# Row scatters issued behind GpSimd's product, and a tail of expert slots without conditions

## The chip, the cores and the metric

The kernel runs on one core of one Trainium2 chip. A core has five engines with instruction queues of their own: TensorE (PE, matrix products), VectorE (DVE), ScalarE (ACT), GpSimd (POOL) and SyncE (SP, which here issues DMAs). They meet through semaphores. The metric is the time of one execution on the device in microseconds, and the kernel before takes 1265.65 us (median of three runs, 1261.61 to 1265.8).

## The reference

Attention that keeps only the 32 largest scores of each row, and behind it a mixture of eight experts of which every row uses one:

```python
batch, heads, seq, dim = 8, 8, 576, 64
scores = (q @ k.T) / sqrt(dim)
kth    = 32nd largest score of each row
scores = where(scores >= kth, scores, -1e9)
x      = softmax(scores) @ v                  # 4608 rows of 512

logits = x @ w_gate + modality_bias[modality_id]
e      = argmax(logits)                       # one of 8 experts per row
gate   = softmax(logits)[e]
out    = gate * (relu(x @ w1[e]) @ w2[e])     # w1: 512x1024, w2: 1024x512
```

How many rows an expert gets is known only while the kernel runs.

## The kernel before, in words

**Attention.** The scores are worked off in 288 tiles of 128 query rows by 576 keys, 36 tiles for each of the eight batches. A Python loop over steps `i` writes the program; the work of one tile is spread over a dozen steps, and in each step every engine gets its share for another tile. There are no due times: what stands in an engine's queue is the order in which this loop calls the functions.

In a step, DVE first merges the candidates of the tile before (L386 to L388), between them takes the eight largest values of seven slices of a new tile (L375, the line with most time on DVE), looks through a product that GpSimd made (`find`, L417), picks the 32nd value of three tiles in every third step (L424 to L426, below a "pick step"), and ends with `keep` (L437): the comparison of the scores with the 32nd value times their exponentials, 128x576, into `P`. The first instruction of a step on DVE is therefore the L386 MAX8, and the time from one L386 MAX8 to the next is the length of a step.

GpSimd in a step: `gate` (L460) reads one number of the `P` that `keep` wrote at the end of the step before, and so holds the queue back until then; `pool_y` (L413) multiplies the scores by a sign mask `K` into `y`, 128x576, which DVE's `find` takes in the next step; `below` (L400) waits for DVE's merge L388 and makes a number that ACT needs for the next mask. In every third step `small` (L394) follows, and in one step of nine `fill` (L325).

**Rows on their way to the experts.** When a batch has its attention output, `route` chooses each row's expert and `send` (L590) scatters the rows to a buffer `xs` in HBM, grouped by expert: five indirect DMAs on GpSimd's queue for each batch, `send` of a first piece, a pause, of the second, and so on, so one in each of five steps. Each is followed by a one-element memset (L516). They are handed out through the list `side`, which a step empties (up to four entries, or up to a pause) together with DVE's small work: ahead of the step's `gate` and `pool_y`. Only the first batch goes through the list `sends` at the end of a step.

**Experts.** 256 rows of one expert make a slot. During attention PE gets matrix products of slots between those of attention (`moe`), after a budget per step (`STEP`) that is written out by the program and knows nothing of the run. A slot's result goes to the output by two more indirect DMAs on GpSimd, `put` (L792), which are issued two steps after the result, from the list `puts` at the end of a step.

**The tail.** What is left after attention are whole slots on PE (`slot`): 8 x 12 products for the hidden layer (L997), 2 x 24 for the output (L1013), a scaling on ACT into `ot` (L1018) and a scatter on GpSimd (L1019) for each half. `slot(n)` computes slot n-1 and fetches and prepares slot n: it loads rows and weights, splits them in two parts, and transposes the rows (L968) between the halves. One slot is computed before the conditions begin. Then the number of slots that are left, `nrem`, is read into a register of every engine (L1289), and 25 nested conditions (L1290) follow, each with a slot in it; a last slot that fetches nothing stands behind them. In this input 19 slots have rows, numbers 0 to 18: the first 13 run beside attention, and 13 to 18 in the tail. So four conditions hold, and the fifth does not: there every engine jumps over the bodies of 21. At the end the condition `bad > 0` (L1365) guards a slow version of the whole kernel, for inputs in which the search for the 32nd value fails; it isn't run here.

Of the kernel before, what the change touches and what calls it, by code (L numbers as in the profile page):

```python
# [12 lines left out]
I32 = mybir.dt.int32  # L13
AF = mybir.ActivationFunctionType
OP = mybir.AluOpType
# [57 lines left out]
def kernel(  # L73
# [12 lines left out]
    nc = tc.nc  # L86
    V, A, G, PE, SP = nc.vector, nc.scalar, nc.gpsimd, nc.tensor, nc.sync
    B, H, S, D = q.shape
    E, Dm, F = w1.shape
    N = B * S  # L90
# [5 lines left out]
    SLOT = 256  # L96
    LCAP = N + SLOT
    MAXSLOT = -(-N // SLOT) + E - 1

    const = ctx.enter_context(tc.tile_pool(name="const", bufs=1))  # L100
# [16 lines left out]
    PAUSE = lambda: None  # L117
# [292 lines left out]
    def pool_y(i):  # L410
        t = T[i]
        t["y"] = wk.tile([128, S], FT, name="y", bufs=YB)
        G.tensor_tensor(t["y"], t["S"], t["K"], op=OP.mult)  # L413
# [408 lines left out]
    side = deque()  # L822
    rush = deque()
    moe = deque()
    sends = deque()
    puts = deque()
    avs = deque()
    xev = deque()
    seen = [0]
    nslot = [0]  # L830

    def ready(n, whole):
        pick, rows, done, tok = sched(n, whole)
        for f in pick + done + rows + tok:
            f()
        for g in range(4):
            load_w1(n, g)
        for g in range(4):
            load_w2(n, g)
# [66 lines left out]
    bd_ = const.tile([128, 4], FT, name="bad")  # L906
# [73 lines left out]
    def choose(s):  # L980
        pick, rows, done, tok = sched(s, False)
        later[s] = rows + tok
        for f in pick + done:
            f()
# [4 lines left out]
    def slot(n):  # L989

        if n is not None:
            fetch(n)
        for f in range(FC):
            ps = acc([128, SLOT])
            for c in range(KC):
                for x, (a, b) in enumerate(TERMS):
                    PE.matmul(ps, w1s[a][:, c, f * 128:(f + 1) * 128], xgs[b][:, c, :],  # L997
                              start=(c == 0 and x == 0), stop=(c == KC - 1 and x == 2))
            A.activation(hs[0][:, f, :], ps, AF.Relu)
            V.scalar_tensor_tensor(hs[1][:, f, :], ps, 0.0, hs[0][:, f, :].bitcast(FT), op0=OP.max, op1=OP.subtract)  # L1000
            if f % 2 == 0:
                split_w2(f // 2)
            if n is not None:
                if f == 0:
                    for g in range(4):
                        load_w1(n, g)
                if f % 2 == 0:
                    load_w2(n, f // 2)
        for t in range(2):
            py = acc([128, Dm])  # L1010
            for f in range(FC):
                for x, (a, b) in enumerate(TERMS):
                    PE.matmul(py, hs[a][:, f, t * 128:(t + 1) * 128], w2s[b][:, f, :],  # L1013
                              start=(f == 0 and x == 0), stop=(f == FC - 1 and x == 2))
                if t == 0 and f % 2 == 1 and n is not None:
                    split_w1(f // 2)
            ot = const.tile([128, Dm], FT, name="ot", bufs=2)
            A.activation(ot, py, AF.Copy, scale=gt[:, t:t + 1])  # L1018
            apart(G.indirect_dma_start(  # L1019
                out=out[:, :], out_offset=bass.IndirectOffsetOnAxis(ap=tk[:, t:t + 1], axis=0),  # L1020
                in_=ot, in_offset=None, bounds_check=N - 1, oob_is_err=False), outs)
            if t == 0 and n is not None:
                turn_rows(n)
                choose(n + 1)
        if n is not None:
            of_rows(n)

# [19 lines left out]
    store = []  # L1047
    for i in range(LAST):
# [62 lines left out]
        if 0 <= b1 < B:  # L1111
            if r == 0:
                chore.extend(recip(b1, den[b1 % 2]))
            rl, rx = (RL, RX) if FAST <= b1 < B - 1 else (RLF, RXF)
            if r == rl[0]:
                rows_of[b1] = logits(b1, xTs(b1))
                cost += COST["logits"]
            if r == rl[1]:
                logit_rows(b1, rows_of[b1], lgb[b1 % 2])
                cost += COST["xrow"]  # L1120
            if r in rx:
                xrow(b1, rx.index(r), xTs(b1), x5)
                cost += COST["xrow"]
            if r == rl[1] + 2:
                steps, store = route(lgb[b1 % 2], bias_all[:, b1], ohb[b1 % 2], x5, int(0 < b1 < B - 1))
                side.extend(steps)

                def done(n=b1 + 1):
                    seen[0] = n * S
                    fresh.clear()  # L1130
                if b1 == 0:
                    side.extend([store.pop(), done])
            if r == max(rl[1], rx[4]) + (1 if b1 == 0 else 2):
                if b1 == 0:
                    sends.extend(f for f in store if f is not PAUSE)
                else:
                    side.extend(store + [done])
        u = i - (TL + 1)
        if avs:
            c, f = avs.popleft()  # L1140
            f()
            cost += c
        if ok(u) and role(u) in (3, 7, 8):
            f = av(u // 9, role(u), xTs(u // 36)[(u // 9) % HP])
# [13 lines left out]
        while seen[0] and spare_pe > 0:  # L1158
# [4 lines left out]
            c, f, new = moe[0]  # L1163
# [25 lines left out]
        for x in range(RN if rush else 0):  # L1189
            f = rush.popleft() if rush else PAUSE  # L1190
# [6 lines left out]
        for x in range(SN - len(small_)):  # L1197
            f = side.popleft() if side and not rush else PAUSE
# [10 lines left out]
        if ok(i) and len(c_) > 1:  # L1209
            n = min(len(c_) - 1, HOLD)  # L1210
# [11 lines left out]
            gate(i - 1 - LR)  # L1222
        if ok(i - LY):
            pool_y(i - LY)
        if ok(i - 1):
            below(i - 1)
        if ok(i - 2) and (i - 2) % 3 == 2:
            small(i - 4)
        if j == 5 and p + 1 < NPAIR:
            fill(p + 1, qbd[(p + 1) % 2])  # L1230
        if sends and seen[0]:
            sends.popleft()()
        for x in puts:
            x[0] -= 1
        while puts and puts[0][0] <= 0:
            puts.popleft()[1]()
        if i == CLOSE:
            alone[0] = True
            S0 = nslot[0]
# [15 lines left out]
        rush.popleft()()  # L1255
    while side:
        side.popleft()()


    while moe:  # L1260
# [12 lines left out]
        first.popleft()()  # L1273
    of_rows(S0)
    choose(S0 + 1)
    nl = const.tile([1, E], FT, name="nl")
    ni = const.tile([1, E], I32, name="ni")
    ns = const.tile([1, 1], FT, name="ns")
    V.tensor_tensor(nl, base[0:1, :], roff[0:1, :], op=OP.subtract)
    V.tensor_scalar(ni, nl, float(SLOT - 1), None, op0=OP.add)  # L1280
    V.tensor_scalar(ni, ni, SLOT.bit_length() - 1, None, op0=OP.arith_shift_right)
    V.tensor_copy(nl, ni)
    V.tensor_reduce(ns, nl, axis=AX.X, op=OP.add)
    nremi = const.tile([1, 1], I32, name="nrem")
    V.tensor_copy(nremi, ns)
    slot(S0 + 1)

    bad = nc.values_load(badi[:, :], min_val=0, max_val=256)
    nrem = nc.values_load(nremi[:, :], min_val=0, max_val=MAXSLOT)  # L1289
    with ExitStack() as nest:  # L1290
        for x in range(MAXSLOT):
            nest.enter_context(tc.If(nrem > x))
            slot(S0 + 2 + x)
    slot(None)
    att.close()

# [22 lines left out]
    def slow():  # L1319
        Pb[:] = [wk.tile([128, 2 * S], FT, name=f"P{i}", bufs=1) for i in range(2)]  # L1320
        outs.clear()
        PR.clear()
        reset_state()
        for x in (scat, reads, fresh):
            x.clear()
        with tc.For_i(0, B, 1) as b:
            dn = den[0]
            sb = wk.tile([128, 1, 5, E], FT, name="sl_b", bufs=1)
            bias_of(*load_mod(b, 1), 1, sb)
            for hp in range(HP):  # L1330
                load(hp, "kqv", b)
                for part in "tkq":
                    prep(hp, part)
                    flush()
                fill(hp, qbd[0])
                for j in range(9):
                    qk(j, hp, qbd[0])
                    sevac(j)
                    r = role(j)
                    slow_tile(j, dn[:, hp, r:r + 1])  # L1340
                    trans(j)
                    evac(j)
                    if r in (3, 7, 8):
                        for _, f in av(hp, r, xTs(0)[hp]):
                            f()
                        xev.popleft()()
            for f in recip(0, dn):
                f()
            L = logits(0, xTs(0))
            while xev:  # L1350
                xev.popleft()()
            logit_rows(0, L, lgb[0])
            flush()
            for c in range(5):
                xrow(0, c, xTs(0), x5)
                flush()
            for part in route(lgb[0], sb[:, 0], ohb[0], x5):
                for f in part:
                    f()
        with tc.For_i(0, MAXSLOT, 1):  # L1360
            ready(0, False)
            for _, f, _ in expert(0, True, False, False, False):
                f()

    with tc.If(bad > 0):  # L1365
        slow()


# [28 lines left out]
```

## Time and profile before

| | |
|---|---|
| median of three runs | 1265.65 us |
| the profiled execution | 1264.55 us |
| span of its trace | 1262.9 us |
| PE busy | 1179.7 us, 93% |
| DVE busy | 1145.9 us, 91% |
| ACT busy | 990.4 us, 78% |
| POOL busy | 681.4 us, 54% |
| granted PE clock, mean | 0.975 |

The span runs from the first to the last instruction; the profiled execution took 1.65 us more than its span. PE and DVE are both busy nearly all the time, but not in the same stretches: attention ends at about 1060 us, behind it DVE has little to do, and from 1105 to 1222 us PE is busy without a gap. Busy shares over the whole span say nothing about which of the two sets the time in a stretch; that is read from what they wait for. A row of a timeline gives the start, the length, the engine, the line, the operation and its tiles, and in brackets how long the engine had been idle before it and what ended that.

### The profile page before, as it was taken

To read this page: it belongs to the slowest core of one execution; us is meant where nothing else is said; L and a number is where in the kernel's file an instruction comes from. 1 tells how busy PE (TensorE), PEld (TensorE's weight loads), DVE (VectorE), ACT (ScalarE), POOL (GpSimd) and SP (SyncE) were. 2 spreads that over 40 slices of the span, in tenths; PEclk is the share of its full clock that TensorE was granted. 3 is DMA by queue.
4 is the path that set the end of the run, shared out by engine and by line. 5 is a ranking of instruction groups with operands and counts; after the bars stand their busy time and mean duration, and the time that the engine had idled before them with its cause. 6 is when DMAs were issued, how large, how long until landed. Compare 5 with 4: busy or idle time off the path is not lost. (4 is left out here: it accounts for less than half of the span.)

```text
span 1262.9 us, 28647 instructions
## 1 busy us (share of the span) xinstructions
PE 1179.7 (93%) x7962; PEld 923.5 (73%) x7962; DVE 1145.9 (91%) x5914; ACT 990.4 (78%) x2014; POOL 681.4 (54%) x1253
## 2 busy tenths in 40 slices
PE   8888888999988999999999999999999999999985
PEld 6667666777766777677777777787778775699885
DVE  6999999999999999999999999999999995477751
ACT  4999987889888988888889888988889875256442
POOL 5888866555574557554755566546655572210110
PEclk6999998999999999999999999999999999999998
DMA  4663337655356755655556666666666524577550
GB/s 100 156 185 84 85 84 199 175 154 161 84 134 183 207 132 148 182 149 151 176 152 182 161 182 163 183 167 176 171 185 176 140 67 133 187 254 270 179 174 15
DMA packets 204340, 197.26 MB, mean 156 GB/s; under 512 B 104413, under 2 KB 151533, under 8 KB 204160
## 3 DMA queue, kind: packets, MB, share of 16 engines
q1 hardware_dynamic: 196880, 175.92, 50.7%
q0 software_dynamic: 6080, 19.00, 4.1%
q8 instruction: 69, 1.13, 0.4%
q14 instruction: 111, 0.91, 0.2%
q10 hardware_dynamic: 1200, 0.30, 0.1%
HBM read 118.63 MB, written 24.23 MB: 113 GB/s over the span
## 5 line engine op out<-in xcount | busy, mean ns | idle before, releaser
L375 DVE MAX8 cand<-Ssb 128x8 f32<-128x82 f32 (+1 forms) x2016 | 433.1, 233 | 5.5 <-ACT Ssb L368 5.5
L413 POOL TENSOR_TENSOR y<-Ssb,K 128x576 f32<-128x576 f32 x288 | 369.7, 1284 | 4.3 <-ACT K L407 4.0
L407 ACT ACTIVATE K<-Ssb,n 128x576 bf16<-128x576 f32 x288 | 227.3, 789 | 36.1 <-POOL y L413 35.0
L363 PE MATMUL S<-ks,qs 128*128 128x288 f32 x992 | 221.8, 346 | 25.7 <-ACT Ssb L368 24.2
L368 ACT ACTIVATE Ssb<-S 128x576 f32<-128x576 f32 x284 | 185.6, 654 | 73.5 <-PE S L363 31.6
L417 DVE MAX8 mg<-y 128x8 f32<-128x576 f32 x288 | 215.1, 747 | 5.5 <-POOL y L413 5.5
L765 PE MATMUL E<-xgT,w1b 128*128 128x256 f32 x816 | 199.9, 388 | 11.3 <-ACT hT L769 9.1
L363 PEld LDWEIGHTS S<-ks,qs 128*128 128x128 f32 x992 | 151.8, 191 | 75.5 <-ACT Ssb L368 41.7
L437 DVE SCALAR_TENSOR_TENSOR P<-Ssb,kth,ex 128x576 f32<-128x576 f32 x230 | 201.8, 877 | 1.6 <-ACT ex L431 1.3
L431 ACT ACTIVATE ex<-Ssb,sm 128x576 f32<-128x576 f32 x256 | 199.9, 781 | 0.0
L479 ACT ACTIVATE PT<-T 128x640 f32<-128x640 f32 (+1 forms) x288 | 190.7, 662 | 6.4 <-PE T L471 6.4
L777 PE MATMUL E<-w2b,hT 128*128 128x512 f32 x400 | 187.3, 597 | 2.1 <-ACT hT L769 2.0
L765 PEld LDWEIGHTS E<-xgT,w1b 128*128 128x128 f32 x816 | 150.7, 193 | 36.5 <-ACT hT L769 12.2
L471 PE MATMUL T<-idf,P 128*128 128x128 f32 x1152 | 170.9, 276 | 6.1 <-ACT P L456 5.8
L460 POOL TENSOR_SCALAR spare<-P 1x1 f32<-1x1 f32 x230 | 46.7, 203 | 203.4 <-DVE mg L386 184.6
L499 PE MATMUL X<-PT,vm 128*64 128x256 f32 (+1 forms) x1536 | 147.1, 334 | 2.8 <-ACT st L277 1.5
L471 PEld LDWEIGHTS T<-idf,P 128*128 128x128 f32 x1152 | 138.0, 142 | 14.9 <-ACT P L456 10.4
L400 POOL TENSOR_SCALAR n<-mg 128x1 f32<-128x1 f32 x288 | 72.4, 251 | 106.1 <-DVE mg L388 98.2
L499 PEld LDWEIGHTS X<-PT,vm 128*64 128x64 f32 x1536 | 88.7, 138 | 48.6 <-issue 10.7
L777 PEld LDWEIGHTS E<-w2b,hT 128*128 128x128 f32 x400 | 70.6, 190 | 63.0 <-issue 57.7
L1019 POOL DMA_INDIRECT out_dram<-ot,tk x12 | 12.0, 998 | 105.0 <-ACT ot L1018 105.0
L903 PE MATMUL E<-onesb 128*128 128x256 bf16 x412 | 61.9, 292 | 2.8 <-ACT K L407 1.6
(234 smaller groups left out, 2231.5 us busy)
## 6 DMA issues: line engine op xcount, KB each, us to landing
w1b<-in_moe_w_dram SPq DMA_DIRECT2D x76, 512.0 KB
w2b<-in_moe_w_dram SPq DMA_DIRECT2D x76, 512.0 KB
ks<-st SPq DMA_DIRECT2D x62, 288.0 KB
ks<-st SPq DMA_DIRECT2D x62, 256.0 KB
qs<-st SPq DMA_DIRECT2D x124, 128.0 KB
xg<-xs SPq DMA_DIRECT2D x19, 516.0 KB
km<-in_k_dram SPq DMA_DIRECT2D x64, 128.0 KB
vm<-in_v_dram SPq DMA_DIRECT2D x32, 256.0 KB
```

The costliest lines, as they stand in the source:

```text
L363: PE.matmul(ps[:, hf, :288], l, m, start=(n == 0), stop=(n == len(terms) - 1))
L375: return [lambda s=s: V.max(c[:, s * 8:s * 8 + 8], T[i]["S"][:, bnd[s]:bnd[s + 1]]) for s in range(NSUB)]
L407: A.activation(t["K"], t["S"], AF.Sign, scale=2.0 ** -24 - 1.0, bias=t["n"][:, 1, i % 3:i % 3 + 1], accum_out=t["n"][:, 0, i % 3:i % 3 + 1])
L413: G.tensor_tensor(t["y"], t["S"], t["K"], op=OP.mult)
L417: V.max(t["mg"][:, i % 3, 24:32], t["y"])
L431: A.activation(t["ex"], t["S"], AF.Exp, bias=t["s"][:, i % 3:i % 3 + 1])
L437: V.scalar_tensor_tensor(t["P"], t["S"], kth[:, i:i + 1], t["ex"], op0=OP.is_ge, op1=OP.mult, accum_out=dn)
L471: PE.transpose(T[i]["pt"][:, x, :], (Pm if c == 4 else Pb[c % 2])[:, h * 512 + x * 128:h * 512 + x * 128 + 128], idf)
L479: A.activation(o, T[i]["pt"][:, :n], AF.Copy)
L499: PE.matmul(o.rearrange("p (a b) -> p a b", a=2) if j < 8 else o, l, r, start=(c == 0), stop=(c == 4))
L765: PE.matmul(ps[:, f % 2], w1b[:, c, f * 128:(f + 1) * 128], xgT[:, c, :], start=(c == 0), stop=(c == KC - 1))
L777: PE.matmul(o["py"], hT[:, f, t * 128:(t + 1) * 128], w2b[:, f, :], start=(f == 0), stop=(f == FC - 1))
```

## The change

Two edits. The first concerns GpSimd's queue in attention: the scatters of batches 1 to 7 are no longer issued where `side` hands them out, but put in a list `posted`, and one entry of `posted`, `sends` or `puts` is issued in a step, right behind `pool_y` and ahead of `below`. So a `put` that is due in the steps of the scatters comes after them.

The second concerns the tail: slots up to number 18 (`SURE`) are written out without a condition. Behind the last slot one condition, `more > 0`, guards a loop over the slots that could be left and, in it, the slow version; `more` is the number of rows that are left plus `bad`. The computation is the same.

```diff
+    posted = deque()
...
-                choose(n + 1)
+                if n < SURE:
+                    choose(n + 1)
...
-                    side.extend(store + [done])
+                    side.extend([f if f is PAUSE else (lambda f=f: posted.append(f)) for f in store[:-1]] +
+                                [store[-1], done])
...
         if ok(i - LY):
             pool_y(i - LY)
+        for x in puts:
+            x[0] -= 1
+        if posted:
+            posted.popleft()()
+        elif sends and seen[0]:
+            sends.popleft()()
+        elif puts and puts[0][0] <= 0:
+            puts.popleft()[1]()
         if ok(i - 1):
             below(i - 1)
         if ok(i - 2) and (i - 2) % 3 == 2:
             small(i - 4)
         if j == 5 and p + 1 < NPAIR:
             fill(p + 1, qbd[(p + 1) % 2])
-        if sends and seen[0]:
-            sends.popleft()()
-        for x in puts:
-            x[0] -= 1
-        while puts and puts[0][0] <= 0:
-            puts.popleft()[1]()
...
+    SURE = max(N // SLOT, S0 + 1)
+    for n in range(S0 + 1, SURE):
+        slot(n)
     nl = const.tile([1, E], FT, name="nl")
...
+    V.tensor_tensor(ns, ns, bd_[0:1, 3:4], op=OP.add)
+    morei = const.tile([1, 1], I32, name="more")
+    V.tensor_copy(morei, ns)
+    slot(SURE)
     bad = nc.values_load(badi[:, :], min_val=0, max_val=256)
-    nrem = nc.values_load(nremi[:, :], min_val=0, max_val=MAXSLOT)
-    with ExitStack() as nest:
-        for x in range(MAXSLOT):
-            nest.enter_context(tc.If(nrem > x))
-            slot(S0 + 2 + x)
+    more = nc.values_load(morei[:, :], min_val=0, max_val=N + 256)
     slot(None)
...
-    with tc.If(bad > 0):
-        slow()
+    with tc.If(more > 0):
+        with tc.For_i(0, MAXSLOT - SURE - 1, 1):
+            ready(0, False)
+            for _, f, _ in expert(0, True, False, False, False):
+                f()
+        with tc.If(bad > 0):
+            slow()
```

On GpSimd's queue, the steps in which batch 5 is scattered, before (L460 is `gate`, L413 the product, L400 `below`, L590 a scatter of rows, L792 a scatter of results):

```order
L590 DMA xs<-x_152,dest 38912x516
L516 MEMSET spare 1x1
L460 TENSOR_SCALAR spare<-P_119 1x1
L413 TENSOR_TENSOR y<-Ssb,K 128x576
L400 TENSOR_SCALAR n<-mg 128x1
L792 DMA out_dram<-ot,stok_130 4608x512
L516 MEMSET spare 1x1
L590 DMA xs<-x_152,dest 38912x516
L516 MEMSET spare 1x1
L460 TENSOR_SCALAR spare<-P_119 1x1
L413 TENSOR_TENSOR y<-Ssb,K 128x576
```

The same steps of the changed kernel:

```order
L460 TENSOR_SCALAR spare<-P_119 1x1
L413 TENSOR_TENSOR y<-Ssb,K 128x576
L590 DMA xs<-x_152,dest 38912x516
L516 MEMSET spare 1x1
L400 TENSOR_SCALAR n<-mg 128x1
L460 TENSOR_SCALAR spare<-P_119 1x1
L413 TENSOR_TENSOR y<-Ssb,K 128x576
L590 DMA xs<-x_152,dest 38912x516
L516 MEMSET spare 1x1
L400 TENSOR_SCALAR n<-mg 128x1
```

The first scatter moved from ahead of `gate` to between the product and `below`, and the scatter of results no longer stands in these two steps. The queues of PE, DVE, ACT and SP are the same in both kernels up to the tail.

On PE's queue, the place of the fifth condition, which does not hold here; behind it in the program stand 21 bodies, and then the slot that fetches nothing. Before:

```order
L1013 MATMUL X<-w2l,hh 128x512
L1013 MATMUL X<-w2h,hl 128x512
L1290 COMPARE_AND_BRANCH
L997 MATMUL X<-xgh,w1h 128x256
L997 MATMUL X<-xgl,w1h 128x256
...
L1013 MATMUL X<-w2h,hl 128x512
L1290 UNCONDITIONAL_BRANCH x26
L997 MATMUL X<-xgh,w1h 128x256
```

And in the changed kernel, between the slot that fetches number 18 and the one that fetches nothing:

```order
L1014 MATMUL X<-w2l,hh 128x512
L1014 MATMUL X<-w2h,hl 128x512
L1294 TENSOR_LOAD badi
L1295 TENSOR_LOAD more
L998 MATMUL X<-xgh,w1h 128x256
L998 MATMUL X<-xgl,w1h 128x256
```

The jump between the two slots is gone, and two register loads, which stood ahead of the first condition, stand in its place. The remaining conditional jump of the tail, over the loop and the slow version, comes behind the last product, where the one over the slow version was.

## Rows read from the trace of the kernel before

**Rows 1.** Stretches: start:end, length, busy us (and instructions) of PE, PEld, DVE, ACT, POOL, ...
```profile
349.20:481.00 131.80, 120.74 (x853) 93.50 (x852) 129.76 (x712) 113.32 (x232) 75.43 (x143) 0.97 0.61 165
618.00:749.70 131.70, 128.23 (x856) 98.28 (x855) 130.91 (x704) 114.69 (x236) 78.61 (x153) 1.00 0.61 169
749.70:881.00 131.30, 129.19 (x865) 99.58 (x864) 129.20 (x704) 114.70 (x238) 79.61 (x153) 1.00 0.61 170
```

**Rows 2.** Groups of DVE, 349.2 to 1045 us: busy us, mean ns | idle before, releaser
```profile
L437 DVE SCALAR_TENSOR_TENSOR P<-Ssb,kth,ex 128x576 f32<-128x576 f32 x168 | 144.2, 858 | 0.0
L417 DVE MAX8 mg<-y 128x8 f32<-128x576 f32 x189 | 141.5, 749 | 5.5 <-POOL y L413 5.5
```

**Rows 3.** Timeline of DVE, first instruction of a step: start, length, line, tiles
```profile
480.83 0.21 DVE L386 MAX8 mg<-cand 128x8 f32<-128x56 f32 x1
...
500.74 0.21 DVE L386 MAX8 mg<-cand 128x8 f32<-128x56 f32 x1
...
877.84 0.21 DVE L386 MAX8 mg<-cand 128x8 f32<-128x56 f32 x1
...
897.17 0.21 DVE L386 MAX8 mg<-cand 128x8 f32<-128x56 f32 x1
...
911.74 0.21 DVE L386 MAX8 mg<-cand 128x8 f32<-128x56 f32 x1
...
924.81 0.21 DVE L386 MAX8 mg<-cand 128x8 f32<-128x56 f32 x1
...
928.45 0.21 DVE L386 MAX8 mg<-cand 128x8 f32<-128x56 f32 x1
...
934.73 0.22 DVE L386 MAX8 mg<-cand 128x8 f32<-128x56 f32 x1
...
938.75 0.22 DVE L386 MAX8 mg<-cand 128x8 f32<-128x56 f32 x1
```

**Rows 4.** Timeline of POOL, 876 to 897 us, where batch 5 is scattered
```profile
876.70 0.19 POOL L400 TENSOR_SCALAR n<-mg 128x1 f32<-128x1 f32 x1 [1.00 <-DVE mg L388]
877.16 1.68 POOL L590 DMA_INDIRECT xs<-x,dest  x1 [0.28 <-issue]
...
879.18 1.27 POOL L413 TENSOR_TENSOR y<-Ssb,K 128x576 f32<-128x576 f32 x1
...
884.03 1.81 POOL L413 TENSOR_TENSOR y<-Ssb,K 128x576 f32<-128x576 f32 x1
...
895.34 1.28 POOL L413 TENSOR_TENSOR y<-Ssb,K 128x576 f32<-128x576 f32 x1
```

**Rows 5.** Timeline of DVE in the same stretch
```profile
877.11 0.80 DVE L437 SCALAR_TENSOR_TENSOR P<-Ssb,kth,ex 128x576 f32<-128x576 f32 x1
...
885.88 0.76 DVE L417 MAX8 mg<-y 128x8 f32<-128x576 f32 x1 [0.44 <-POOL y L413]
...
895.41 1.83 DVE L437 SCALAR_TENSOR_TENSOR P<-Ssb,kth,ex 128x576 f32<-128x576 f32 x1
```

**Rows 6.** Timeline of all engines, 482 to 485 us
```profile
482.60 0.98 POOL L590 DMA_INDIRECT xs<-x,dest  x1 [0.21 <-DVE cand L375]
...
483.24 0.80 DVE L437 SCALAR_TENSOR_TENSOR P<-Ssb,kth,ex 128x576 f32<-128x576 f32 x1
```

**Rows 7.** Timeline of ACT in the tail: the scaling of each half of a slot
```profile
1129.03 0.69 ACT L1018 ACTIVATE ot<-X,gt 128x512 f32<-128x512 f32 x1 [4.68 <-issue]
1146.10 0.69 ACT L1018 ACTIVATE ot<-X,gt 128x512 f32<-128x512 f32 x1 [1.38 <-PE X L1013]
...
1222.34 0.69 ACT L1018 ACTIVATE ot<-X,gt 128x512 f32<-128x512 f32 x1 [4.59 <-issue]
1244.34 0.69 ACT L1018 ACTIVATE ot<-X,gt 128x512 f32<-128x512 f32 x1 [5.16 <-PE X L1013]
```

**Rows 8.** Timeline of PE, the start of the last slot
```profile
1225.44 0.39 PE L997 MATMUL X<-xgh,w1h 128*128 128x256 f32 x1 [3.19 <-ACTq L1290]
```

**Rows 9.** Instructions of line 1290: queue, count, ns min/median/max, first and last start
```profile
L1290 PEldq COMPARE_BRANCH  x6: 65/76/3425, 1126.0 to 1222.4; - x6
```

More of the change, by code (lines that the diff above doesn't have):

```diff
@@ L1257 @@
         side.popleft()()
+        while posted:
+            posted.popleft()()
     while moe:
@@ L1275 @@
     choose(S0 + 1)
+    SURE = max(N // SLOT, S0 + 1)
+    for n in range(S0 + 1, SURE):
+        slot(n)
     nl = const.tile([1, E], FT, name="nl")
-    ni = const.tile([1, E], I32, name="ni")
     ns = const.tile([1, 1], FT, name="ns")
     V.tensor_tensor(nl, base[0:1, :], roff[0:1, :], op=OP.subtract)
-    V.tensor_scalar(ni, nl, float(SLOT - 1), None, op0=OP.add)
-    V.tensor_scalar(ni, ni, SLOT.bit_length() - 1, None, op0=OP.arith_shift_right)
-    V.tensor_copy(nl, ni)
     V.tensor_reduce(ns, nl, axis=AX.X, op=OP.add)
-    nremi = const.tile([1, 1], I32, name="nrem")
-    V.tensor_copy(nremi, ns)
-    slot(S0 + 1)
+    V.tensor_tensor(ns, ns, bd_[0:1, 3:4], op=OP.add)
+    morei = const.tile([1, 1], I32, name="more")
+    V.tensor_copy(morei, ns)
+    slot(SURE)
     bad = nc.values_load(badi[:, :], min_val=0, max_val=256)
-    nrem = nc.values_load(nremi[:, :], min_val=0, max_val=MAXSLOT)
-    with ExitStack() as nest:
-        for x in range(MAXSLOT):
-            nest.enter_context(tc.If(nrem > x))
-            slot(S0 + 2 + x)
+    more = nc.values_load(morei[:, :], min_val=0, max_val=N + 256)
     slot(None)
```

## The prediction

> **What bounds the kernel now.** I read the table of stretches first, then the groups of DVE by line with what they wait for, and then the timelines of DVE and GpSimd beside each other in the steps of the scatters; for the tail the timelines of ACT and PE.
>
> In attention DVE and PE are both nearly full. Between 349.2 and 481 us PE idles 131.80 - 120.74 = 11.1 us, but one period of a batch later in the run, 749.7 to 881 us, has 131.30 - 129.19 = 2.1 us of idle PE and as much of idle DVE [rows 1]. So who sets the pace is read from the waits. DVE waits for nothing in its large lines but in `find`, 5.5 us, all for GpSimd's product [rows 2]. And `keep` takes 858 ns on average over 168 tiles [rows 2], where an undisturbed one takes 0.80 us [rows 5]. These two are GpSimd's mark on DVE, and I looked for where they stand.
>
> They stand in the steps of the scatters. Five steps in a row with two pick steps among them take 928.45 - 911.74 = 16.71 us where nothing is scattered [rows 3]. The five steps with the scatters of batch 5, of the same kinds, take 897.17 - 877.84 = 19.33 us, and those of batch 2 take 500.74 - 480.83 = 19.91 us [rows 3]. That is 2.6 and 3.2 us too much, and these are the ends: batches 1 to 6 all lie between them. Batch 0 is scattered in steps that DVE fills with other work, batch 7 behind attention.
>
> How it happens is in the two timelines. GpSimd waits 1.00 us for DVE's merge before it can run `below` [rows 4]; the scatter behind it comes too late and starts at 877.16, just after `keep` (877.11) [rows 4, 5]. It takes 1.68 us, where one that began 0.64 us ahead of `keep` took 0.98 and left `keep` at 0.80 [rows 6]. `gate` and the product wait behind it, so the product starts at 879.18, 1.34 us into the step that began at 877.84, where `gate` alone would hold it back a few tenths. From then on GpSimd is behind: with a scatter of results and another of rows in the queue its products start at 884.03 and, in this batch, last at 895.34 [rows 4]. DVE pays twice: `find` waits (0.44 us at 885.88), and a `keep` that meets a product in progress takes 1.83 us (895.41) [rows 5].
>
> **The skill on this.** Rows 5 and 6 show that a scatter begun within `keep` is held up and one begun before it isn't. The Trainium skill, in "SBUF — State Buffer", section "Who interferes with whom", says that a DVE instruction with two SBUF inputs contends with a GpSimd one that reads SBUF, that the second to issue blocks, and, as an inference from a probe with `tensor_tensor`, that such an instruction does not hold up the writing of descriptors. With the first part the product and `keep` agree (1.83 against 0.80 us). By the second the scatter at 877.16 should have taken about 1.0 us and took 1.68, so the measurement decides. By that rule the sum would be the same, the scatters would be harmless wherever they start, and the slower case below would fall away; by the row it stays.
>
> **What the change does to GpSimd's queue.** It takes the scatter from between `below` and `gate`, and puts it between the product and `below`, where GpSimd idled 1.00 us anyway [rows 4]. `gate` then runs as soon as `keep` has ended, the product (1.27 us) from about 0.3 to 1.6 us of the step, the scatter, 0.28 us later and 0.98 long, from about 1.9 to 2.9 [rows 4, 6]. `keep` starts 877.84 - 877.11 = 0.73 us ahead of the next step [rows 3, 5]; a short step, (16.71 - 2 x 3.64) / 3 = 3.14 us by rows 3, has it at 2.4. So the scatter starts ahead of `keep`, the harmless order of rows 6, by 0.5 us. What is queued behind it: `below`, which now meets `keep` and runs after it, then `gate`, which would have waited for the end of `keep` in any case. ACT needs the number of `below` two steps later. The cost of that I take as 0.8 us in all (30 scatters, some 0.03 us each of a late `gate` on steps where it matters), bounded by 0 and by 30 x 0.2 us.
>
> **Price on DVE.** Six batches at 2.6 to 3.2 us make 6 x 2.9 = 17.4 us. As a check, 168 x (0.858 - 0.80) = 9.7 us of long `keep` and 5.5 us of waits are 15.2 [rows 2, 5]; the rest is in the short instructions of pick steps.
>
> **Who is late next.** PE. In the later batches it has only 2.1 us of idle time per period [rows 1], less than the 2.6 to 3.0 that DVE gives back, and its queue is the same. In 618 to 749.7 us it has 131.70 - 128.23 = 3.5, before that more. So I count 3.0 us for each of batches 1 to 3 and 2.1 for each of 4 to 6: 3 x 3.0 + 3 x 2.1 = 15.3 us. That PE can give up all of its idle time is the open part; bounds are 0 and 17.4 us.
>
> **The scatters of results** move too, and leave room ahead of `gate`. A step behind one takes 938.75 - 934.73 = 4.02 us, where a pick step takes 928.45 - 924.81 = 3.64 [rows 3], so 0.4 us each; I found six such steps, up to 2.4 us. In the later batches PE has nothing left to give for them, so I take 1.0 us, between 0 and 2.4. Those that move behind the scatters of rows wait up to five steps; nothing is queued for them but one of two buffers `ot`, which the next half but one needs many steps later.
>
> Attention: 15.3 + 1.0 - 0.8 = 15.5 us.
>
> **The tail.** PE sets it: from one half's scaling to the next the four slots under true conditions read alike, and PE has no gap. A condition that holds costs PE 65 to 76 ns of its queue, hidden; the one that fails 3425 ns [rows 9]. There the first product of the last slot comes 3.19 us late [rows 8], and the slot then runs slowly at first. Both together are in the distance of two scalings: in an ordinary slot the first half comes 1146.10 - 1129.03 = 17.07 us after the slot before, in the last slot 1244.34 - 1222.34 = 22.00 us [rows 7]. The difference, 4.9 us, goes, since the two slots now follow each other as the others do. The register loads that take its place stood ahead of the slot that gave 17.07, so they cost PE nothing there. What follows the last product, with the jump over what isn't run, is as before. DVE loses the choice of a slot that nobody needs and gets four tiny instructions one slot earlier; it waits for PE there, so I take nothing. Bounds: 3.2 us (the gap alone) and 4.9.
>
> **Sum.** 15.5 + 4.9 = 20.4 us. The profiled execution took 1264.55 us (span 1262.9), so 1244.15, and I say 1244 us. The profiled execution is 1.1 us under the median of 1265.65, within the spread of the runs.
>
> **Rivals.**
> PE takes over sooner. Part of its idle time may come from elsewhere (its own waits for ACT), and then about half of the attention gain stays: 1264.55 - 4.9 - 8 = 1251.7. For it: DVE and PE are equally full in 749.7 to 881 us [rows 1]. Against: no group of DVE waits for scores, so PE is ahead of it and has something to lose before it decides.
>
> The scatters cost the same in their new place, because `below` and `gate` are now late instead of the product: only the tail is won, 1259.7 us. For it: GpSimd's work in a step is the same. Against: it had 1.00 us of idle time exactly there.
>
> Slower: the scatter meets `keep` again, now in every step. If the product ends later than about 2.1 us into a short step, the scatter starts inside `keep`, takes 1.68 instead of 1.0, the next product runs into the next `keep`, and that takes 1.83 instead of 0.80. At 1.0 us for each of 30 scatters, in place of the 17.4 us of today, attention loses 12.6, and with the tail the time is 1264.55 + 12.6 - 4.9 = 1272 us. It decides at 0.5 us of lag, and pick steps, which are 0.5 us longer, take back as much in every third step; that is why I hold it unlikely.
>
> **Numbers.** Forecast as worked out, 1238 to 1249 us: 0.70. PE takes over sooner: 0.17. Only the tail: 0.09. Slower: 0.04. The lower end is everything at its bound, 1264.55 - 17.4 - 2.4 - 4.9 = 1239.9, less the spread of runs. The range of 1238 to 1257 leaves out the slower case and most of the tail's. A difference of 0.5%, 6.3 us, is about what can be told from no change: faster means under 1259.3. All of the first two and a little of the third lie there: 0.88. The same: 0.08. Slower: 0.04.
>
> **What would show it.** Right: five steps of scatters at about 16.7 us; no wait of `find` for the product; `keep` at 0.8 us on average; the product always starting about 0.3 us into a step; the periods of the later batches near 129 us; ACT's two scalings across the last boundary 17.1 us apart, and no idle PE there. Wrong: scatters of 1.3 to 1.7 us, or long `keep`s in the same steps; a period still at 131 us with idle DVE, which waits for scores (PE has taken over); or a jump of several us on PE that is now in another place of the tail.

## The result and the profile after

The changed kernel takes 1252.89 us (median of six runs, 1247.69 to 1254.05), the kernel before beside it 1265.33 us: ratio 0.9896, 95% interval 0.9875 to 0.9917, or 12.4 us less. The span went from 1262.9 to 1251.1 us. The forecast was 1244 us, a gain of 20.4 us: the sign held and both parts of the change gained, but 8 us of the gain are missing.

**What came as foreseen.** The stretches of the two periods between the starts of the scatters (columns as in [rows 1]):

```profile
616.60:746.77 130.17, 127.69 (x854) 98.43 (x851) 129.38 (x704) 113.96 (x237) 77.58 (x153) 1.00 0.64 171
746.77:877.53 130.76, 128.61 (x861) 98.83 (x860) 129.32 (x706) 113.42 (x236) 77.60 (x153) 1.00 0.64 171
```

They are 1.5 and 0.5 us shorter than the two later rows of [rows 1]; 2.1 us and more were expected. Yet the scatters themselves show the full gain. In the timeline of DVE these are the starts of the five steps of batch 5 and of the one after them, with the `keep` of the second:

```profile
874.39 0.21 DVE L386 MAX8 mg<-cand 128x8 f32<-128x56 f32 x1
...
877.53 0.22 DVE L386 MAX8 mg<-cand 128x8 f32<-128x56 f32 x1
...
880.43 0.82 DVE L437 SCALAR_TENSOR_TENSOR P<-Ssb,kth,ex 128x576 f32<-128x576 f32 x1
...
881.17 0.22 DVE L386 MAX8 mg<-cand 128x8 f32<-128x56 f32 x1
...
884.32 0.22 DVE L386 MAX8 mg<-cand 128x8 f32<-128x56 f32 x1
...
887.46 0.21 DVE L386 MAX8 mg<-cand 128x8 f32<-128x56 f32 x1
...
891.10 0.21 DVE L386 MAX8 mg<-cand 128x8 f32<-128x56 f32 x1
```

The steps take 3.14, 3.64, 3.15, 3.14 and 3.64 us, together the 16.71 us that [rows 3] give for five steps without a scatter, and no `find` among them waits. GpSimd's timeline in the first of them shows why:

```profile
874.78 1.27 POOL L413 TENSOR_TENSOR y<-Ssb,K 128x576 f32<-128x576 f32 x1
876.22 1.07 POOL L590 DMA_INDIRECT xs<-x,dest  x1 [0.17 <-issue]
```

The product starts 0.39 us into the step instead of 1.34 [rows 4], and the scatter takes 1.07 us instead of 1.68.

The tail is as foreseen too: ACT's two scalings at the boundary that [rows 7] showed at 22.00 us, and the branch behind the last slot, now in line 1367 (columns as in [rows 9]):

```profile
1215.66 0.69 ACT L1019 ACTIVATE ot<-X,gt 128x512 f32<-128x512 f32 x1 [4.61 <-issue]
1232.73 0.69 ACT L1019 ACTIVATE ot<-X,gt 128x512 f32<-128x512 f32 x1 [5.22 <-PE X L1014]
```
```profile
L1367 PEldq COMPARE_BRANCH  x1: 3360/3360/3360, 1233.8 to 1233.8; - x1
```

They are 17.07 us apart, 4.93 less. The jump of 3.4 us is still there, but in the program behind PE's last product; it ends at 1237.2 us and that product at 1238.0, so no work comes later for it.

**Where the rest went.** The groups of DVE over attention, counterpart of [rows 2]:

```profile
L417 DVE MAX8 mg<-y 128x8 f32<-128x576 f32 x191 | 143.0, 749 | 2.1 <-POOL y L413 2.1
L437 DVE SCALAR_TENSOR_TENSOR P<-Ssb,kth,ex 128x576 f32<-128x576 f32 x169 | 137.0, 811 | 0.0
```

The waits of `find` should have been gone: 2.1 us are left here, and over the whole span there are 6.8, where before had 5.5. Their releaser is the product, so GpSimd is still late somewhere. Of its groups one idles for a reason that was not there before, `fill` (L325): twice 64 partitions of queries copied for the next pair of heads, in one step of nine. The view of one line, first of before, then of after, with what ended its idle time:

```profile
L325 POOLq EVENT_SEMAPHORE  x30: 17/43/43, 205.8 to 963.6; - x30
...
  DVE ks L272: 3.9, 1
  DMA xs<-x,dest: 0.2, 1
```
```profile
L325 POOLq EVENT_SEMAPHORE  x30: 17/43/5035, 205.9 to 994.4; - x30
...
  DMA out_dram<-ot,stok: 14.5, 6
  issue: 8.5, 3
  DMA xs<-x,dest: 5.0, 1
```

So 28 us of waiting in GpSimd's queue, in ten places, for scatters ("issue" is a wait for which the trace shows no releaser). One such place, in the timeline of GpSimd: before, then after.

```profile
863.14 1.27 POOL L413 TENSOR_TENSOR y<-Ssb,K 128x576 f32<-128x576 f32 x1
864.75 0.19 POOL L400 TENSOR_SCALAR n<-mg 128x1 f32<-128x1 f32 x1 [0.34 <-DVE mg L388]
865.02 0.67 POOL L325 TENSOR_SCALAR qbd<-st 64x128 fp32r<-64x128 f32 x2
865.97 1.26 POOL L792 DMA_INDIRECT out_dram<-ot,stok  x1 [0.28 <-POOL qbd L325]
```
```profile
858.54 1.28 POOL L413 TENSOR_TENSOR y<-Ssb,K 128x576 f32<-128x576 f32 x1
859.99 1.06 POOL L792 DMA_INDIRECT out_dram<-ot,stok  x1 [0.17 <-ACT K L407]
...
861.81 0.29 POOL L325 TENSOR_SCALAR qbd<-st 64x128 fp32r<-64x128 f32 x1
864.14 0.30 POOL L325 TENSOR_SCALAR qbd<-st 64x128 fp32r<-64x128 f32 x1 [2.03 <-DMA out_dram<-ot,stok]
864.52 0.18 POOL L460 TENSOR_SCALAR spare<-P 1x1 f32<-1x1 f32 x1
864.67 1.27 POOL L413 TENSOR_TENSOR y<-Ssb,K 128x576 f32<-128x576 f32 x1
```

Before, the scatter of results stood behind `fill`; the next `fill` came nine steps later and found it landed. Now it stands ahead of it in the same step, and the second half of `fill` starts only 3.09 us after the end of the scatter's instruction (861.05). `gate` and the product behind it come 2.0 us late, and DVE, in the middle of its small routing operations, meets the product:

```profile
864.65 1.35 DVE L613 TENSOR_TENSOR r_pr<-r_pb,ohb 128x40 f32<-128x40 f32 x1
```

Before, the same operation was this row:

```profile
869.27 0.17 DVE L613 TENSOR_TENSOR r_pr<-r_pb,ohb 128x40 f32<-128x40 f32 x1
```

That step lasts 5.19 instead of 4.02 us.

The wait stands in the list of instructions (DMASW are the counters of GpSimd's DMAs), and only at the second of the two. This is another such place, with the second half of its `fill` in the timeline:

```profile
374.28 0.46 POOL L325 TENSOR_SCALAR qbd<-st 64x128 fp32r<-64x128 f32 x1 [3.31 <-DMA out_dram<-ot,stok]
```
```
L792 DMA out_dram<-ot,stok_131 4608x512
L516 MEMSET spare 1x1 [waits Pool_49]
L400 TENSOR_SCALAR n<-mg 128x1 [waits DVE_49]
L325 TENSOR_SCALAR qbd_115<-st 64x2x64
L325 TENSOR_SCALAR qbd_115<-st 64x2x64 [waits DMASW5_49,DMASW4_49,DMASW6_49,DMASW3_49,DMASW7_49,DMASW2_49,Pool_49]
```

Both write the same tile, so the second waits for the first, and with it for the scatters that GpSimd issued earlier. At the place of the timelines above, the list has one counter there, DMASW4, that of the scatter issued just ahead. Before has such waits too, but for scatters that had landed: they cost 0.2 us in all.

As the order of DVE's instructions in attention is the same, its 287 steps can be compared one by one. One of them stands apart, the step that begins at 294.46 us in before. There DVE waits for a product of PE in some executions, also with the attention loop of before (the kernel with the tail alone):

```profile
298.00 0.69 DVE L533 TENSOR_TENSOR x<-X,rd 128x512 f32<-128x512 f32 x1 [1.72 <-PE X L532]
```

Sums of the differences to before, in us:

| steps | forecast | changed | the same again | only scatters of rows moved | fill first | both edits |
|---|---|---|---|---|---|---|
| scatters of rows, 6 x 5 steps | -15.3 | -17.1 | -17.1 | -12.1 | -17.2 | -17.1 |
| behind results with no `fill` beside them, 4 steps | -1.0 | -1.7 | -1.8 | -0.1 | -1.8 | -1.7 |
| around `fill`, 16 steps | 0 | +11.9 | +9.6 | -0.2 | +0.8 | -2.1 |
| the step at 294.46 us | 0 | +0.4 | +1.2 | 0.0 | +1.1 | +1.1 |
| all others | +0.8 | -0.3 | -0.1 | +0.1 | 0.0 | +0.8 |
| attention | -15.5 | -6.8 | -8.2 | -12.2 | -17.1 | -19.0 |

The forecast's 1.0 us was for six steps behind a scatter of results. In two of the six that got shorter, a `fill` stands beside that scatter and the step behind them got longer, so they are counted around `fill`; with both edits they stay short, and nothing is lost behind them.

With 4.9 us of the tail the first column of measurements makes 11.7 us; the spans differ by 11.8.

### The profile page after: what moved, and what is told of

It is laid out like the page before. It is cut to its first block, busy times and chain, and to the rows that moved or that the text cites. A ratio compares the mean times of both kernels' runs of the same rounds, so it can differ in the third digit from the quotient of the medians.

```text
span 1251.1 us, 28550 instructions
## 1 busy us (share of the span) xinstructions
PE 1170.1 (94%) x7962; PEld 915.7 (73%) x7962; DVE 1135.7 (91%) x5890; ACT 987.9 (79%) x2014; POOL 670.7 (54%) x1253
## 4 chain that ended last, share of the span: by engine, by line
DVE 63%; PE 27%; issue 3%; DMA 2%; POOL 2%; ACT 2%; SPq 0%; POOLq 0%; DVEq 0%
DVE cand L375 17%; DVE mg L417 12%; DVE P L437 11%; PE E L777 4%; PE X L1014 4%; DVE cand L386 4%; PE X L998 3%; PE E L765 3%; DVE cand L387 3%; PE X L499 2%; DVE mg L388 2%; DVE mg L386 2%; DVE mg L387 2%; PE S L363 2%; PE T L471 2%
## 5 line engine op out<-in xcount | busy, mean ns | idle before, releaser
L375 DVE MAX8 cand<-Ssb 128x8 f32<-128x82 f32 (+1 forms) x2016 | 434.6, 234 | 5.6 <-ACT Ssb L368 5.6
L413 POOL TENSOR_TENSOR y<-Ssb,K 128x576 f32<-128x576 f32 x288 | 367.7, 1277 | 4.4 <-ACT K L407 4.0
L765 PE MATMUL E<-xgT,w1b 128*128 128x256 f32 x816 | 196.9, 384 | 10.9 <-ACT hT L769 9.2
L437 DVE SCALAR_TENSOR_TENSOR P<-Ssb,kth,ex 128x576 f32<-128x576 f32 x230 | 192.9, 839 | 1.5 <-ACT ex L431 1.2
L460 POOL TENSOR_SCALAR spare<-P 1x1 f32<-1x1 f32 x230 | 42.0, 182 | 194.7 <-DVE mg L386 177.4
L400 POOL TENSOR_SCALAR n<-mg 128x1 f32<-128x1 f32 x288 | 75.2, 261 | 98.6 <-DVE mg L388 88.7
L386 DVE MAX8 mg<-cand 128x8 f32<-128x56 f32 x288 | 61.9, 215 | 0.2
```

Of the source, the lines that this page charges most:

```text
L375: return [lambda s=s: V.max(c[:, s * 8:s * 8 + 8], T[i]["S"][:, bnd[s]:bnd[s + 1]]) for s in range(NSUB)]
L437: V.scalar_tensor_tensor(t["P"], t["S"], kth[:, i:i + 1], t["ex"], op0=OP.is_ge, op1=OP.mult, accum_out=dn)
L765: PE.matmul(ps[:, f % 2], w1b[:, c, f * 128:(f + 1) * 128], xgT[:, c, :], start=(c == 0), stop=(c == KC - 1))
```

## The experiments

The theory: the gain is what the forecast said, and `fill`'s second instruction, which waits for the landing of the scatter ahead of it, takes about 10 us of it back. The rivals: PE takes the gain back, as the likeliest rival of the forecast said (1251.7 us, close to what was measured); or the scatters of results collide by themselves.

**Only the scatters of rows moved.**

```diff
-        for x in puts:
-            x[0] -= 1
         if posted:
             posted.popleft()()
-        elif sends and seen[0]:
-            sends.popleft()()
-        elif puts and puts[0][0] <= 0:
-            puts.popleft()[1]()
...
             fill(p + 1, qbd[(p + 1) % 2])
+        if sends and seen[0]:
+            sends.popleft()()
+        for x in puts:
+            x[0] -= 1
+        while puts and puts[0][0] <= 0:
+            puts.popleft()[1]()
```

> The changed kernel, but only the scatters of rows stay behind GpSimd's product; the scatters of results (sends, puts) go back to the end of the step, behind fill, as before. Theory (fill's second instruction waits for the landing of a DMA that is issued ahead of it in its step): ten of the eleven waits of 1.6 to 5.0 us in front of L325 vanish; the one of batch 0 at 213 us stays, since a scatter of rows causes it. DVE's waits of find at 310, 376, 769 and 900 us go, the steps that lost 1 to 2 us are back at before's length, and those with a put keep what it cost before (about 0.4 us each). Time 1243 to 1247 us, about 7 us under the changed kernel. Rival 1 (TensorE becomes the bound and takes the gain back): the waits at L325 go, but the time stays within 2 us of the changed kernel (1251 to 1254), with DVE or ACT waiting for PE in the same batches. Rival 2 (the puts behind the product cost by themselves, by colliding with the step's two-input VectorE operations): the time is 1243 to 1247 as well, which the next two runs tell apart.

Measured: 1249.59 us, ratio 0.9878 (0.9863 to 0.9893). The waits in front of `fill` are gone, even the one of batch 0 (1.3 us are left), and so are the losses around it. But the time is 3 us above the expectation, since the steps of the scatters give only 12.1 us and the results nothing. In each of the six batches a `put` stands at the end of the first of the five steps and holds up the product in the second; timeline of GpSimd, then of DVE:

```profile
743.47 1.01 POOL L792 DMA_INDIRECT out_dram<-ot,stok  x1 [0.27 <-DVE mg L386]
744.49 0.09 POOL L516 MEMSET spare<- 1x1 f32 x1
744.67 0.18 POOL L460 TENSOR_SCALAR spare<-P 1x1 f32<-1x1 f32 x1
744.82 1.28 POOL L413 TENSOR_TENSOR y<-Ssb,K 128x576 f32<-128x576 f32 x1
```
```profile
745.18 0.96 DVE L424 TENSOR_TENSOR eq<-i9s,n 128x27 f32<-128x27 f32 x1
```

The step takes 4.43 us; in the changed kernel, where that `put` queues behind the scatters of rows, it takes 3.64 and L424 0.17. So the rival of colliding scatters of results is wrong and its opposite holds: their move is worth 5.0 + 1.7 = 6.7 us, and costs 8 to 12 around `fill` in the four traces of this loop.

**`fill` in one instruction**, with a mask of zeros and ones; it stays behind the scatter.

```diff
+    half_ = const.tile([128, 2, 64], FT, name="half")
+    G.memset(half_, 0.0)
+    for h in range(2):
+        G.memset(half_[h * 64:h * 64 + 64, h, :], 1.0)
...
-        for h in range(2):
-            r = slice(h * 64, h * 64 + 64)
-            G.tensor_scalar(bd[r, :, r], PR[p]["st"][r, :, 1, 512:]..., 1.0, 1.0, ...)
+        G.tensor_tensor(bd..., PR[p]["st"][:, :, 1, 512:]..., half_..., op=OP.mult)
```

> The changed kernel with all its scatters behind the product; fill is one product with a mask of zeros and ones instead of two copies of 64 partitions, so it has no second instruction that waits for everything GpSimd issued before. Theory: no wait in front of fill for a landing, also at 213 us; all eleven losing steps are back at before's length and the puts behind the product keep their small gains; attention ends about 20 us earlier than before: time 1238 to 1243 us. Rival 1 (TensorE is the bound): 1250 to 1253 us, and the waits appear on DVE with PE behind them. Rival 2 (the puts collide by themselves): the steps with a put and fill lose 1 us still, 1248 to 1252 us.

Measured: 1242.78 us, ratio 0.9819 (0.9807 to 0.9832). `fill` waits for nothing any more after the start of the kernel:

```profile
L327 POOL TENSOR_TENSOR qbd<-st,half x31: 727/741/1403, 26.6 to 986.3; 128x256 fp32r<-128x256 f32 x31
```

It stands where it stood, behind the same scatters, and what is gone is the dependence between its halves: in the list of instructions it waits for no counter of a DMA any more. That settles what the wait hangs on. Against 2 x 0.30 us it is a little longer, and some steps lose 0.3 us. The profiled execution, at 1245.8 us, is the slowest of its five; in it the 16 steps around `fill` are as long as before (-0.1 us), and attention is 14.2 us shorter.

**`fill` ahead of the scatter**, between the product and the scatter.

```diff
         if ok(i - LY):
             pool_y(i - LY)
+        if j == 5 and p + 1 < NPAIR:
+            fill(p + 1, qbd[(p + 1) % 2])
...
         if ok(i - 2) and (i - 2) % 3 == 2:
             small(i - 4)
-        if j == 5 and p + 1 < NPAIR:
-            fill(p + 1, qbd[(p + 1) % 2])
```

> The changed kernel, but fill stands ahead of the step's DMA on GpSimd, right behind the product. Theory: fill waits only for DMAs of earlier steps, which have landed; its idle in front is under 0.5 us at all places but perhaps where two steps in a row issue a DMA; time 1239 to 1245 us. Rival 1 (TensorE is the bound): 1250 to 1253 us. Rival 2 (the puts collide by themselves): 1248 to 1252 us, the steps with a put and fill still longer than before's by about 1 us.

Measured: 1244.99 us, ratio 0.9839 (0.9826 to 0.9851), attention 17.1 us shorter than before. Of the idle time in front of `fill` 3.2 us are left, more than expected. Three steps are still 0.7 to 0.9 us too long: `fill` and the scatter together push the next product into DVE's routing operations. Timelines of DVE and of GpSimd:

```profile
888.51 1.13 DVE L655 TENSOR_SCALAR s_oh<-s_key,s_m 128x8 f32<-128x8 f32 x1
```
```profile
886.64 1.06 POOL L792 DMA_INDIRECT out_dram<-ot,stok  x1 [0.45 <-DVE cand L375]
...
888.34 1.27 POOL L413 TENSOR_TENSOR y<-Ssb,K 128x576 f32<-128x576 f32 x1
```

**No scatter in a step with a `fill`.**

```diff
-        if posted:
+        if j == 5 and p + 1 < NPAIR:
+            pass
+        elif posted:
```

> The changed kernel, but in the steps that have a fill no scatter is issued (of rows or of results); it goes one step later. Theory (fill's second instruction waits for the landing of a DMA that is issued just ahead of it): no idle over 0.5 us in front of L325, none of the eleven steps longer than before's, and also none of the three of 0.9 us that fill ahead of the DMA still had; periods of the later batches 128 to 128.8 us; time 1240 to 1244 us, 1 to 4 us under the kernel with fill ahead of the DMA (1245.0). Rival (TensorE sets the later batches at about 129.1 us): the steps are short again, the period stays at 129.0 to 129.5 and the time within 1 us of 1245.0.

Measured: 1244.26 us, ratio 0.9836 (0.9817 to 0.9855). The long steps are gone, but the last scatter of batch 0 now goes a step later, and DVE waits 3.13 us for the rows gathered behind it, where it waited 1.47 before (this run, then before):

```profile
218.41 0.17 DVE L694 COPY sgt<-xg 128x2 f32<-128x2 f32 x1 [3.13 <-DMA xg<-xs]
```
```profile
218.09 0.17 DVE L694 COPY sgt<-xg 128x2 f32<-128x2 f32 x1 [1.47 <-DMA xg<-xs]
```

The two later periods are 128.39 and 129.78 us, and in the second DVE waits twice for PE, 0.62 and 0.51 us. So the time, 0.7 us under that of `fill` first, lies in the range of this run's rival and 0.3 us above that of its theory: the run shows that the long steps go, and does not tell whether PE limits the later batches.

**The kernel before with `fill` behind the scatters of results**, the converse test:

```diff
-        if j == 5 and p + 1 < NPAIR:
-            fill(p + 1, qbd[(p + 1) % 2])
         if sends and seen[0]:
             sends.popleft()()
...
             puts.popleft()[1]()
+        if j == 5 and p + 1 < NPAIR:
+            fill(p + 1, qbd[(p + 1) % 2])
```

> The kernel before, with one edit: fill stands at the end of the step, behind the scatters of results instead of ahead of them. Theory: this alone makes the wait. In the steps with a fill and a scatter of results (about ten) fill's second instruction idles 1.5 to 4 us, the next gate and product are late, and the time rises by 6 to 14 us, to 1271 to 1280. Rival (fill's wait only costs where the scatters also stand behind the product): the idle appears in front of L325, but the time stays within 3 us of before (1263 to 1269).

Measured: 1274.71 us beside 1264.28 for before, ratio 1.0082 (1.0060 to 1.0104): 10.4 us slower by this edit alone. The view of L325:

```profile
L325 POOLq EVENT_SEMAPHORE  x30: 17/43/3873, 207.7 to 1007.0; - x30
...
  DVE cand L375: 6.1, 3
...
  DMA out_dram<-ot,stok: 3.3, 2
```

Attention is 8.2 us longer in the trace, 6.0 of it in the 16 steps around `fill`; 1.1 are in the steps of the scatters of rows, and the kernel with the tail alone, whose attention loop is before's, has 1.2 there too. DVE named as a releaser of `fill` here is the case in which the last releaser in the records isn't the one that was waited for: L375 does not write what `fill` reads.

**The two parts apart, and the changed kernel again.** One kernel takes the tail alone, one the attention loop alone; the third is the changed kernel, unedited.

> The kernel before with the new tail alone: the scatters stay where they were. All theories: the chain of the tail is 17.1 instead of 22.0 us from slot to slot at the one place, the rest is before's: 4.5 to 5.5 us faster than before, 1260 to 1261 us. If the two parts of the change don't add (the tail's gain hangs on where attention ends), it is more than 1 us off that.

> The changed kernel's attention loop with the tail of before. All theories: the tail's 4.9 us come back and nothing else, 1256 to 1259.5 us; in front of L325 the same idle of 25 to 30 us as in the changed kernel. If it is under 1254 or over 1262, the two parts of the change don't add.

> The changed kernel as it is, beside the others on the same chip: 1251 to 1255 us by every theory, with the idle in front of L325 (25 to 30 us in all) in the same steps.

Measured: the tail alone 1262.71 us, ratio 0.9967 (0.9955 to 0.9979), 2.7 to 5.7 us; attention alone 1254.55 us, ratio 0.9922 (0.9900 to 0.9943), which is 3.0 above the changed kernel beside it, at 1251.56, ratio 0.9893 (0.9874 to 0.9912). The product of the two ratios, 0.9889, is within that interval, so the parts add. But the expectations of both parts missed by 1.5 to 1.7 us. In the traces ACT's two scalings are 17.07 us apart with the new tail and 21.92 with the old, so the tail's 4.9 us are in each execution, but attention of one and the same loop differs by a few us from execution to execution: the profiled one with the tail alone needed 3.5 us more than before's (in the step that begins at 294 us in before, its DVE waited 1.7 us for a product of PE, before's not at all), and the changed kernel waited 5.04 us in front of `fill` at 213 us in one execution and 2.2 in another.

**Both edits on `fill`**: ahead of the scatter, and no scatter of results in its step; scatters of rows stay allowed there.

```diff
+        if j == 5 and p + 1 < NPAIR:
+            fill(p + 1, qbd[(p + 1) % 2])
...
         if posted:
             posted.popleft()()
+        elif j == 5 and p + 1 < NPAIR:
+            pass
         elif sends and seen[0]:
...
-        if j == 5 and p + 1 < NPAIR:
-            fill(p + 1, qbd[(p + 1) % 2])
```

> The changed kernel with fill ahead of the step's DMA, right behind the product, and no scatter of results in a step that has a fill; scatters of rows stay allowed there. Theory: it has neither the steps of 4.8 to 5.0 us of the kernel with fill ahead of the DMA (three, 0.9 us each) nor the later scatter of batch 0 that made DVE wait 3.1 us for gathered rows in the kernel with no scatter in those steps; 2 us under both, 1241 to 1243.5 us. Rival (from here TensorE sets the pace, its waits move into the evictions of its products): 1244 to 1245 us, with DVE waiting for X from PE in more places than before.

> The changed kernel as it is, on the same chip as the one before it: 1251 to 1254 us by every theory.

Measured: 1241.64 us, ratio to before 0.9808 (0.9787 to 0.9828); the changed kernel beside it 1251.40, ratio to before 0.9888 (0.9869 to 0.9908). That is the lowest time here, though its interval overlaps with that of `fill` in one instruction, so the two are not told apart. Its later periods:

```profile
739.13:867.45 128.32, 127.78 (x860) 98.71 (x859) 127.53 (x706) 112.89 (x235) 76.53 (x153) 1.00 0.63 174
867.45:996.58 129.13, 128.59 (x864) 99.39 (x863) 127.75 (x704) 113.71 (x237) 76.30 (x153) 1.00 0.60 168
```

The first is 3.0 us shorter than the 131.30 of [rows 1]. Here PE comes in sight: it idles 0.54 us in each, and in the second DVE waits 0.51 us for a product of PE (L533). So PE would be next from about 128 to 129 us a period, an estimate from these two rows, but not at 130.8, where the changed kernel stood.

## Why the prediction was right, and where it was not

- **Scatters of rows behind the product: right, its size a little low.** 17.1 us, near the 17.4 before the cut for PE. The cut to 15.3 was wrong. In the changed kernel it was not put to the test, since its later periods got shorter by only 1.5 and 0.5 us. With both edits on `fill` one period got 3.0 us shorter, though [rows 1] show PE idle for 2.1. PE's busy time fell too, from 129.19 to 127.78 us, but so did the matrix products in the records, from 865 to 860; whether a part of the busy time was waiting for others is not shown.
- **Scatters of results: this step failed.** "nothing is queued for them but one of two buffers `ot`", and so a small gain, 1.0 us. In the four steps with no `fill` beside them the gain was 1.7 us, about the 0.4 us each that the forecast had read before it cut the sum to 1.0 for PE's sake. But the forecast named what waits for the buffer and not what waits on GpSimd's own queue for everything that this queue issued; `fill` does not occur in it. `fill` stands in the same step, and its second half waits for the landing: 8 to 12 us around it, 11.9 in the profiled execution, which the last scatter of batch 0 (one of rows) shares in. `fill` first, `fill` in one piece, and no scatter beside it each bring the 7 to 10 us back; the converse edit costs 10.4 in the kernel before.
- **`below` and `gate` late, 0.8 us: not seen.** The other steps sum to -0.1 to -0.3 in the two traces of the table.
- **The tail: right,** 4.9 us.
- **PE takes over: refuted for the changed kernel,** though its 1251.7 us lay next to the measured time. A rival's number that fits is not its mechanism. "Only the tail" and the slower case did not occur either: `keep` is at 0.80 to 0.82 in the scatter steps.

Without `fill`'s wait the sum comes out: with `fill` first the kernel takes 1244.99 us beside 1265.83, 20.8 us less where 20.4 were forecast. Its parts do not agree as well: the scatters gave 1.9 and 0.8 us more than forecast, `below` and `gate` cost none of their 0.8, and the step at 294.46 us and the steps around `fill` took 1.8 back.

## What to carry to other kernels

When an asynchronous operation is issued earlier in a queue, look not only for who needs its result, but for every later instruction of that queue that waits for an earlier one of the same queue: such a wait can take in the landing of all DMAs issued ahead of it. In this kernel two instructions that write parts of one tile made such a wait; one instruction, or a place ahead of the DMA, avoided it. And when a time lands on a rival's number, look for the wait that this rival names before believing it.

## What the runs showed of the hardware

- A scatter on GpSimd's queue takes 1.06 us as an instruction (859.99), but what waited for its landing started 3.09 us after its end; at another place, 898.37 us, it was 4.3 us after. The Trainium skill, "DMA: Bandwidth & Descriptors", section "Anatomy of one DMA — SWDGE (gpsimd) path", puts a fixed cost of about 2 us mostly down to the confirmation that the last byte has landed. These waits agree in kind and are longer.
- Small operations of DVE are held until GpSimd's product ends: 128x40 with two inputs 1.35 us instead of 0.17 (it began at 864.65 and ended with the product, at 866.0), 128x27 0.96, and a TENSOR_SCALAR of 128x8 1.13. The Trainium skill, "SBUF — State Buffer", section "Who interferes with whom", has the first two as the case of two SBUF inputs, and the trace agrees.
- A scatter that began within DVE's `keep` took 1.03 to 1.68 us in the trace of before, 1.41 in the median of 14; the 64 others took 0.91 to 1.13. In the changed kernel one of 78 began within a `keep`, and it took 1.59.
